# The opening of a fused Fourier-mixing and ELU kernel: x in five pieces, smaller bias parts, a new order of table passes and X units

## The chip, the cores and the metric

The kernel runs on one core of a Trainium2 chip. A core has a matrix engine (TensorE, PE in the profile; its weight loads are listed as PEld), VectorE (DVE), ScalarE (ACT), GpSimd (POOL) and a queue engine (SyncE, SP), which work side by side, each through its own list of instructions in order, and wait for one another through semaphores. Transfers between the chip's main memory (HBM) and the on-chip memory (SBUF) run on 16 DMA engines; here they are asked for by SP and by POOL. Matrix products land in PSUM, a small memory from which ACT and DVE copy them out.

The metric is the device time of one execution in microseconds (us); smaller is better. Beside it there is a profile of one execution with a record of every instruction.

## The reference

```python
def _attn_ref(x, w_r, w_i, b_r, b_i):          # x: (8, 3008, 256)
    X = np.fft.rfft(x, axis=1)
    Xr, Xi = (X.real.astype(np.float32), X.imag.astype(np.float32))
    Yr = Xr @ w_r - Xi @ w_i + b_r
    Yi = Xr @ w_i + Xi @ w_r + b_i
    lam = 0.01
    Yr = np.sign(Yr) * np.maximum(np.abs(Yr) - lam, 0.0)
    Yi = np.sign(Yi) * np.maximum(np.abs(Yi) - lam, 0.0)
    Y = Yr.astype(np.float64) + 1j * Yi.astype(np.float64)
    return np.fft.irfft(Y, n=x.shape[1], axis=1).astype(np.float32)

def _moe_ref(x, w_in, w_out):                  # x: (24064, 256), d_ff = 2048
    h = x @ w_in
    g = np.where(h > 0.0, h, np.exp(np.minimum(h, 0.0)) - 1.0)
    return (g @ w_out).astype(np.float32)
```

The second function is applied to the first one's output, all 8 batches of 3008 tokens in one row.

## The kernel before

**Stages.** The Fourier transform over 3008 = 47 x 64 points is made as two steps of matrix products, and so is its inverse. For each batch the work is cut into units:

- A (6 units): the first transform step. A unit multiplies four of x's 24 row groups by the table M1, copies PSUM to a bf16 tile and writes that to a DRAM buffer (DA). Reading it back in another order gives Z: four loads of 384 KB in the first batch.
- X (8 units): the second step. A unit takes eight of Z's 32 slices times eight slices of the table M2 (`[96, 32, 2, 48]`), and copies the result to XT. Units 2g and 2g+1 need quarter g of Z and of M2.
- M (12): the product with the weights (`wcat_r`, `wcat_s`), bias and soft threshold; an M unit reads all of XT.
- B (6), with the table M3, through another DRAM buffer (DB), and Y (8), with the table M4: the inverse.
- Then the feed-forward part: `front` (w_in and the exponential), `elu`, `back` (w_out and the output).

**Order.** The order of instructions is the order in which the program emits them. For batch 0 all stages stand in line (the opening, up to about 56 us); from then on the feed-forward part of batch b runs with the stages of batch b+1 put between its steps (`plan`). In the opening PE is given filler products on a constant tile (`idle_pe`, L295 to L298).

**The tables.** In the opening the tables are calculated while x arrives. M2 is made in four groups g of eight slices, each by the same steps: `points(g)` (DVE: L433 and L434 make the phase index, L443 the sign `st`), `phases(g)` (the phase, on DVE at L453 or on ACT at L449), `wraps(g)` (DVE, L463 and L464: minus the nearest whole turn), `sizes(g)` (ACT, L474: absolute value), `signs(g)` (DVE, L468), `sines(g, 0)` and `sines(g, 1)` (ACT, L478). `slot0` (DVE, L487, four instructions) corrects slice 0. M3 is made of v3 (DVE, L559), w3 (DVE, L599 and L600: the same wrap), a3 (ACT, L606), two sines (ACT, L613) and two products (DVE, L617 and L621).

**Queues around the change.** x comes in six pieces of 512 KB, asked for by POOL between the iotas that fill index tiles. SP asks for the bias rows, then writes the six A results, then asks for `w_r` and `w_i`, then for the four quarters of Z, then for the bias in 128 rows (`bias_bc`) and for the first part of w_in. POOL turns the weights into bf16 (L520 to L523) and behind that asks for batch 1's x and for half of w_out (L597, L598).

**Bias.** Every second M unit adds its bias by a product with `bias_p`, a `[128, 512]` bf16 tile whose rows 0, 32 and 64 hold three bf16 parts of the fp32 bias and whose other rows are zero (L189). It is made from `brow`, `[128, 512]` in fp32, into which the bias rows are loaded three times (L301 to L307), with L601 on ACT and L602 and L607 to L610 on DVE.

**Copies.** `evac` (L123) copies PSUM to SBUF on ACT or on DVE. In the opening the A units are copied by ACT (L127), X units 1, 4 and 7 by DVE (L125), the others by ACT. A and X units use two PSUM buffers in turn. The last copy of the X stage is followed by the first M units (`first_M`), the two sines of M3 and, after five M units, the first B unit (L630).

Of the kernel before, what the change touches and what calls it, by code (L numbers as in the profile page):

```python
# [29 lines left out]
def kernel(  # L30
# [92 lines left out]
    def evac(dst, src, on_dve):  # L123
        if on_dve:
            nc.vector.tensor_copy(dst, src)  # L125
        else:
            nc.scalar.copy(dst, src)  # L127

    def unit_A(b, u, alone=False, on_dve=False, ahead=False):
        ci, uu = u // 2, u % 2  # L130
        if uu == 0:
            if ahead and ci > 0:
                A_of[b, ci] = wk2.tile([P, 8, D], BF16, name="Bz", tag="Bz")
            elif alone:
                A_of[b, ci] = wk4.tile([P, 8, D], BF16, name="A", tag="Bs")
            else:
                A_of[b, ci] = wk2.tile([P, 8, D], BF16, name="A", tag="A")
            if ci == 0:
                DA_of[b] = dram.tile([NJ, P, D], BF16, name="DA", tag="DA")
        xt, A = xts[ci], A_of[b, ci]  # L140
        dav = DA_of[b].rearrange("j p d -> p j d")
        ps = unit_ps("aps", alone or ahead)
        for j in range(2):
            nc.tensor.matmul(  # L144
                ps[:, j, :], lhsT=M1[:],
                rhs=xt[:, 4 * uu + 2 * j : 4 * uu + 2 * j + 2, :], start=True, stop=True,
            )
        evac(
            A[:, 4 * uu : 4 * uu + 4, :].rearrange("p n d -> p (n d)"),
            ps[:].rearrange("p a b -> p (a b)"), on_dve,  # L150
        )
        j0 = 8 * ci
        if alone:
            j0 += 4 * uu
            nc.sync.dma_start(dav[:, j0 : j0 + 4, :], A[:, 4 * uu : 4 * uu + 4, :])
        elif uu == 1:
            nc.sync.dma_start(dav[:, j0 : j0 + 8, :], A[:])
# [137 lines left out]
    def idle_pe(n):  # L295

        for _ in range(n):
            nc.tensor.matmul(ips[:], lhsT=busy[:, 0:P], rhs=busy[:], start=True, stop=True)  # L298

    brow, rest = (wk3.tile([P, 2 * D], F32, name="yb", tag="yb") for _ in range(2))  # L300
    nc.vector.memset(brow[:], 0.0)  # L301
    for o, bv in ((0, b_r), (D, b_i)):
        for k in range(3):
            nc.sync.dma_start(
                brow[32 * k : 32 * k + 1, o : o + D],
                bass.AP(tensor=bv.tensor, offset=bv.offset, ap=[[0, 1], [1, D]]),
            )  # L307
    idle_pe(9)
    xts = []
    for ci in range(3):  # L310
        xt = constp.tile([P, 8, D], F32R, name=f"xt{ci}")
        xts.append(xt)
    with tc.tile_pool(name="stagep", bufs=1) as stagep:
        def first_x(u):
            load_x(0, u // 2, 4 * (u % 2), 4 * (u % 2) + 4)

        def col(eng, src, s1, op0, s2=None, op1=None, n=1, dt=F32):
            t = stagep.tile([P, n], dt, name=f"c{len(cols)}")
# [49 lines left out]
        for s0, s1 in ((0, 8), (8, NS)):  # L368
            ss = [[15, s1 - s0]]
            iota("", None, ss + [[-15, K1]], base=384 + 15 * s0, out=mi[:, s0:s1, :, 0])  # L370
            if s0:
                first_x(5)
            iota("", None, ss + [[15, K1]], base=15 * s0, out=mi[:, s0:s1, :, 1])
            if s0 == 0:
                iota("", None, [[0, 1], [-15, K1]], base=480, out=mi[:, 0:1, :, 1])
                first_x(3)
                first_x(4)

        m3i = stagep.tile([P, NV], I32, name="m3i")
        k1t = row("k1t", [P, NV])  # L380
# [45 lines left out]
        a2 = row("a2", [P, NS, 2 * K1])  # L426
        r2 = row("r2", [P, 8, 2 * K1])

        def points(g):

            gs, z = slice(8 * g, 8 * g + 8), slice(0, RZ)
            m_, k_ = mi[z, gs], kv[z, gs]
            dve.tensor_scalar(m_, m_, 63, None, ALU.bitwise_and)  # L433
            dve.scalar_tensor_tensor(  # L434
                k_, m_, float(N1), kk1[z].unsqueeze(1).to_broadcast([RZ, 8, K1, 2]),
                ALU.mult, ALU.add,
            )
            if g == 0:
                dve.scalar_tensor_tensor(
                    kv[z, 0, :, 1], mi[z, 0, :, 1], float(N1), kk1[z, :, 0], ALU.mult, ALU.add  # L440
                )
            kf = k_.rearrange("p s k t -> p s (k t)")
            dve.tensor_scalar(st[z, gs], kf, S // 2 + 0.5, -0.5, ALU.is_gt, ALU.add)  # L443

        def phases(g, on_act=False):
            gs, z = slice(8 * g, 8 * g + 8), slice(0, RZ)
# [13 lines left out]
        def wraps(g):  # L460
            gs, z = slice(8 * g, 8 * g + 8), slice(0, RZ)
            v, r = v2[z, gs], r2[z]
            dve.tensor_scalar(r, v, CMAGIC, -CMAGIC, ALU.add, ALU.add)  # L463
            dve.tensor_tensor(v, v, r, ALU.subtract)  # L464
# [33 lines left out]
        pool.tensor_tensor(v4[:], v4[:], r4[:], ALU.subtract)  # L498

        def fA(u):  # L500
            unit_A(0, u, alone=True)
            if u < 5:
                idle_pe(3)

        points(0)
        phases(0)
        wraps(0)
        for u in range(4):
            fA(u)
        points(1)  # L510
        phases(1, True)
        points(2)
        sizes(0)
        fA(4)
        wraps(1)
        signs(0)
        fA(5)
        nc.sync.dma_start(w_r_f[:], w_r.rearrange("(c p) e -> p c e", p=P))
        nc.sync.dma_start(w_i_f[:], w_i.rearrange("(c p) e -> p c e", p=P))
        pool.tensor_copy(wcat_r[:, :, 0:D], w_r_f[:])  # L520
        pool.tensor_copy(wcat_r[:, :, D : 2 * D], w_i_f[:])
        pool.tensor_scalar(wcat_s[:, :, 0:D], w_i_f[:], -1.0, None, ALU.mult)
        pool.tensor_copy(wcat_s[:, :, D : 2 * D], w_r_f[:])  # L523
        for g in range(4):
            load_Z(0, 8 * g, 8 * g + 8)
        for o, bv in ((0, b_r), (D, b_i)):
            nc.sync.dma_start(
                bias_bc[:, o : o + D],
                bass.AP(tensor=bv.tensor, offset=bv.offset, ap=[[0, P], [1, D]]),
            )  # L530
        sines(0, 0)
        sizes(1)
        phases(2, True)
        dve.tensor_scalar(m3i[:], m3i[:], 63, None, ALU.bitwise_and)
        k3 = row("k3", [P, NV])
        dve.scalar_tensor_tensor(k3[:], m3i[:], float(N1), k1t[:], ALU.mult, ALU.add)
        dve.tensor_scalar(sg3[:], k3[:], S // 2 + 0.5, -0.5, ALU.is_gt, ALU.add)
        points(3)
        phases(3)
        wraps(2)  # L540
        signs(1)
        sines(0, 1)
        sines(1, 0)
        sizes(2)
        sines(1, 1)
        wraps(3)
        signs(2)
        slot0()
        sines(2, 0)
        sizes(3)  # L550
        sines(2, 1)
        signs(3)
        sines(3, 0)
        sines(3, 1)


        full = [P, NV, N2]
        k3b = k3[:].unsqueeze(2).to_broadcast(full)
        dve.scalar_tensor_tensor(  # L559
            v3[:], n2row.unsqueeze(1).to_broadcast(full), 1.0 / S, k3b, ALU.mult, ALU.mult  # L560
        )
        idle_pe(40)

    gatep = ctx.enter_context(tc.tile_pool(name="gatep", bufs=2))
    late2 = ctx.enter_context(tc.tile_pool(name="late2", bufs=2))
# [30 lines left out]
    for ci in range(3):  # L596
        load_x(1, ci)  # L597
    load_w_out(0)  # L598
    nc.vector.tensor_scalar(w3[:], v3[:], CMAGIC, -CMAGIC, ALU.add, ALU.add)  # L599
    nc.vector.tensor_tensor(w3[:], v3[:], w3[:], ALU.subtract)  # L600
    nc.scalar.copy(bias_p[:], brow[:])  # L601
    nc.vector.tensor_tensor(rest[:], brow[:], bias_p[:], ALU.subtract)  # L602
    for u in range(8):
        unit_X(0, u, alone=True, on_dve=u in (1, 4, 7))
        if u == 1:
            nc.scalar.activation(a3[:], w3[:], AF.Abs)  # L606
            nc.vector.tensor_copy(bias_p[32:64], rest[32:64])  # L607
            nc.vector.tensor_copy(bias_p[64:P], rest[64:P])
            nc.vector.tensor_tensor(rest[64:P], rest[64:P], bias_p[64:P], ALU.subtract)
            nc.vector.tensor_copy(bias_p[64:P], rest[64:P])  # L610
        idle_pe(1)
    for o, src, sc, bi in ((1, w3, TURN, 0.0), (0, a3, -TURN, hpi[:])):
        nc.scalar.activation(  # L613
# [289 lines left out]
```

## Time and profile before

| | |
|---|---|
| median of 3 runs | 911.97 us (911.74 to 912.75) |
| the profiled execution | 911.1 us |
| its span on the core | 909.3 us |
| TensorE busy | 887.7 us, 98% of the span |
| granted TensorE clock, mean | 0.999 |
| first, last A unit starts on PE | 5.98, 13.22 us |
| first load of Z issued | 18.26 us |
| first, last X unit starts on PE | 22.62, 29.18 us |
| first M, first B unit starts on PE | 30.01, 35.37 us |

A row of the profile's order of time or chain begins with the start and the length in us from the span's start; then come the engine, the line of the kernel and the operation, what is written and read, the tile's shape, and in brackets the idle time of the engine before it and what ended that. A "q" behind an engine's name means its queue, which issues a transfer or waits. In the table by stretches each engine has its busy us and in brackets the number of its instructions; then come the granted clock, the share of the DMA engines' time and GB/s.

### The profile page before, as it was taken

What the parts mean: (1) busy time and instruction counts of PE and PEld (TensorE: products, weight loads), DVE (VectorE), ACT (ScalarE), POOL (GpSimd) and SP (SyncE); (2) the same over time, 40 slices, a digit from 0 to 9 for tenths busy, and PEclk for the clock granted to TensorE, in tenths of its full rate; (3) what the DMA queues carried; (4) which work ended last, traced back from release to release, by engine and by line L of the source; (5) the groups of instructions that cost most, each with busy time, mean ns of one, the idle gap of its engine ahead of it and who ended that gap; (6) DMA issues with size and microseconds to landing.
All of it is one profiled execution on the core that took longest, in us unless ns stands there. A gap on an engine that the chain in (4) does not pass through costs nothing.

```text
span 909.3 us, 17183 instructions
## 1 busy us (share of the span) xinstructions
PE 887.7 (98%) x6622; PEld 652.0 (72%) x6726; DVE 717.0 (79%) x891; ACT 696.6 (77%) x851; POOL 314.7 (35%) x440
## 2 busy tenths in 40 slices
PE   8889999999999999999999999999999999999997
PEld 3457667876688677886678766787667866777775
DVE  8768778877788778797788877888778877778776
ACT  6668788777878778787787788878887877767664
POOL 7600540333321441405404153033332134443664
PEclk9999999999999999999999999999999999999999
DMA  8997116621283215732166032752228111231011
GB/s 270 309 265 232 47 48 186 209 70 47 83 236 123 71 47 142 192 109 82 58 196 199 24 98 60 207 171 70 70 70 232 29 43 47 79 86 48 24 48 47
DMA packets 90670, 106.24 MB, mean 117 GB/s; under 512 B 5270, under 2 KB 81308, under 8 KB 87228
## 3 DMA queue, kind: packets, MB, share of 16 engines
q1 hardware_dynamic: 84332, 77.62, 30.7%
q0 software_dynamic: 5968, 27.26, 9.1%
q8 instruction: 52, 0.85, 0.4%
q14 instruction: 30, 0.25, 0.1%
q10 hardware_dynamic: 288, 0.26, 0.1%
HBM read 55.32 MB, written 49.81 MB: 116 GB/s over the span
## 4 chain that ended last, share of the span: by engine, by line
PE 85%; DVE 5%; ACT 4%; DMA 3%; issue 2%; SPq 1%; POOL 0%; DVEq 0%; ACTq 0%; POOLq 0%
PE ps_o L774 34%; PE hps L716 33%; PE mps L192 9%; PE yps L282 2%; PE bps L244 2%; PE aps L144 2%; PE xps L175 2%; DMA Bs<-DB 2%; DVE gT L743 1%; DVE Et L755 1%; ACT Et L730 1%; ACT Et L727 1%; ACT Bz L257 1%; DVE osb L785 1%; SPq L792 0%
## 5 line engine op out<-in xcount | busy, mean ns | idle before, releaser
L774 PE MATMUL ps_o<-w_out_r,gT 128*128 128x256 f32 x3008 | 477.1, 301 | 0.2 <-DVE gT L741 0.2
L774 PEld LDWEIGHTS ps_o<-w_out_r,gT 128*128 128x128 f32 x3008 | 403.4, 189 | 50.3 <-DVE osb L785 1.3
L716 PE MATMUL hps<-yT,w_in_s 128*128 128x512 bf16 (+7 forms) x1650 | 382.1, 351 | 6.3 <-DVE gT L743 0.9
L741 DVE SCALAR_TENSOR_TENSOR gT<-Et,hps 128x512 fp32r<-128x512 f32 (+1 forms) x274 | 224.0, 847 | 75.8 <-POOL Et L753 38.8
L743 DVE SCALAR_TENSOR_TENSOR gT<-hps,Et 128x1024 fp32r<-128x1024 f32 x197 | 240.9, 1223 | 16.6 <-PE hps L716 1.4
L716 PEld LDWEIGHTS <-w_in_s 128*128 128x128 bf16 x1728 | 141.6, 98 | 129.0 <-issue 22.0
L730 ACT ACTIVATE Et<-hps 128x1024 f32<-128x1024 f32 x197 | 203.0, 1030 | 11.9 <-PE hps L716 5.4
L753 POOL TENSOR_SCALAR Et<-Et 128x512 f32<-128x512 f32 x189 | 112.5, 613 | 221.4 <-ACT Et L725 221.4
L755 DVE TENSOR_SCALAR Et<-Et 128x1024 f32<-128x1024 f32 x197 | 136.2, 691 | 47.4 <-ACT Et L730 40.5
L210 POOL TENSOR_SCALAR clip<-yb 128x512 f32<-128x512 f32 x84 | 51.6, 614 | 315.4 <-DVE yb L202 277.9
L725 ACT ACTIVATE Et<-hps 128x512 f32<-128x512 f32 x190 | 103.2, 595 | 64.7 <-PE hps L716 63.9
L727 ACT ACTIVATE Et<-hps 128x1024 f32<-128x1024 f32 x84 | 86.2, 1026 | 71.7 <-PE hps L716 70.1
L211 POOL TENSOR_TENSOR Y<-yb,clip 128x512 bf16<-128x512 f32 x84 | 107.2, 1276 | 7.0
L728 ACT ACTIVATE Et<-Et 128x1024 f32<-128x1024 f32 x84 | 88.8, 1058 | 2.7
L202 DVE TENSOR_TENSOR yb<-mps,bias_bc 128x512 f32<-128x512 f32 x89 | 61.3, 689 | 35.8 <-PE mps L192 23.9
L127 ACT CAST XT<-xps 128x768 bf16<-128x768 f32 x61 | 48.7, 799 | 16.2 <-PE xps L175 16.2
L127 ACT CAST yT<-yps 128x752 bf16<-128x752 f32 x63 | 49.7, 788 | 13.4 <-PE yps L282 13.3
L192 PE MATMUL mps<-wcat_r,XT 128*128 128x512 bf16 x180 | 55.6, 384 | 0.8 <-ACT Bz L257 0.3
L192 PE MATMUL mps<-wcat_s,XT 128*128 128x512 bf16 x182 | 54.9, 379 | 0.7
L127 ACT CAST A<-aps 128x1024 bf16<-128x1024 f32 x43 | 43.5, 1014 | 13.0 <-PE aps L144 12.3
L192 PEld LDWEIGHTS <-XT 128*128 128x128 bf16 x384 | 30.8, 98 | 29.6 <-DVE XT L125 0.6
L257 ACT CAST Bz<-bps 128x1024 bf16<-128x1024 f32 x46 | 46.0, 999 | 2.1 <-PE bps L244 2.1
(112 smaller groups left out, 413.5 us busy)
## 6 DMA issues: line engine op xcount, KB each, us to landing
xt<-in_x_dram POOLq DMA_DIRECT2D x21, 1024.0 KB, 7.2
out_dram<-osb SPq DMA_DIRECT2D x158, 128.0 KB
Bs<-DB SPq DMA_DIRECT2D x32, 384.0 KB
DB<-Bz SPq DMA_DIRECT2D x21, 512.0 KB
DA<-A SPq DMA_DIRECT2D x19, 512.0 KB
Z<-DA SPq DMA_DIRECT2D x7, 1152.0 KB
Z<-DA SPq DMA_DIRECT2D x11, 384.0 KB
xt<-in_x_dram POOLq DMA_DIRECT2D x6, 512.0 KB, 5.8
```

The costliest lines, as they stand in the source:

```text
L127: nc.scalar.copy(dst, src)
L192: nc.tensor.matmul(ps, lhsT=XT[:, dt, c, o : o + P], rhs=wm[:, dt, :], start=(not biased and m == 0 and dt == 0), stop=(m == 1 and dt == 1),)
L211: nc.gpsimd.tensor_tensor(Y_of[b, q][:, i, :], yb, clip[:], ALU.subtract)
L716: nc.tensor.matmul(hps[:, s, c0:c1], lhsT=w_in_s[:, dt, ft * P : ft * P + P], rhs=yT_of[b][:, dt, t0 : t0 + c1 - c0], start=(dt == 0), sto ...
L725: nc.scalar.activation(E_[:, s], hps[:, s], AF.Exp)
L727: nc.scalar.activation(E_, hps[:], AF.Relu, scale=-1.0)
L730: nc.scalar.activation(E_, hps[:], AF.Exp)
L741: nc.vector.scalar_tensor_tensor(o, e, -1.0, h, ALU.add, ALU.max)
L743: nc.vector.scalar_tensor_tensor(o, h, 0.0, e, ALU.max, ALU.add)
L753: eng.tensor_scalar(E_[:, s], E_[:, s], 1.0, 0.0, ALU.min, ALU.max)
L755: nc.vector.tensor_scalar(E_, E_, 1.0, -1.0, ALU.min, ALU.add)
L774: nc.tensor.matmul(po[q][:, i_ % 2, :], lhsT=gT[:, s, i_ * P : i_ * P + P], rhs=w_out_r[:, ft, :], start=(ft == 0 and i_ % 2 == 0), stop=( ...
```

## The change

All of it is in the opening of batch 0.

- x is asked for in five pieces: two of 1 MB, one of 512 KB, two of 256 KB.
- The last A unit is copied and written in two halves. A unit 3 is copied by DVE.
- The bias is loaded once as 8 rows of 64, split into three bf16 parts of that shape by five small DVE instructions (`split_bias`), written to a DRAM buffer, and read back into rows 0, 32 and 64 of `bias_p` (`place_bias`, three transfers). POOL clears `bias_p` at the very start.
- SP asks for Z's first two quarters, then the weights, then the other two quarters.
- The signs of groups 1 to 3 (`points(g, pool)`) and w3 go to POOL; group 3's `phases` and the negated copy of `w_i` go to ACT.
- The passes over the M2 table are put in another order; `sizes(0)` and what follows now stand behind all A units. X units 0 to 3 are emitted between the passes of groups 2 and 3, and X units 1, 3, 5 and 7 are copied by DVE. a3 stands behind X unit 6. 29 filler products stand ahead of the X units in place of 40.
- The weights' bf16 copies on POOL stand behind all that.

```diff
+        if alone and u == 5:
+            for j in range(2):
+                c = 4 * uu + 2 * j
+                evac(A[:, c : c + 2, :].rearrange("p n d -> p (n d)"), ps[:, j, :], on_dve)
+                nc.sync.dma_start(dav[:, j0 + c : j0 + c + 2, :], A[:, c : c + 2, :])
+            return
...
-    brow, rest = (wk3.tile([P, 2 * D], F32, name="yb", tag="yb") for _ in range(2))
-    nc.vector.memset(brow[:], 0.0)
-    for o, bv in ((0, b_r), (D, b_i)):
-        for k in range(3):
...
+    BR, BC = 8, 2 * D // 8
+    brow, rest = (wk3.tile([BR, BC], F32, name="yb", tag="yb") for _ in range(2))
+    bpart = wk3.tile([BR, 3, BC], BF16, name="yb", tag="yb")
+    bias_d = dram.tile([3, BR, BC], BF16, name="bias_d", tag="bias_d")
+    for o, bv in ((0, b_r), (BR // 2, b_i)):
+        nc.sync.dma_start(
+            brow[o : o + BR // 2, :],
+            bass.AP(tensor=bv.tensor, offset=bv.offset, ap=[[BC, BR // 2], [1, BC]]),
+        )
+    nc.gpsimd.memset(bias_p[:], 0.0)
+    def split_bias():
+        nc.vector.tensor_copy(bpart[:, 0], brow[:])
+        nc.vector.tensor_tensor(rest[:], brow[:], bpart[:, 0], ALU.subtract)
+        nc.vector.tensor_copy(bpart[:, 1], rest[:])
+        nc.vector.tensor_tensor(rest[:], rest[:], bpart[:, 1], ALU.subtract)
+        nc.vector.tensor_copy(bpart[:, 2], rest[:])
+    def place_bias():
+        for k in range(3):
+            nc.sync.dma_start(
+                bias_p[32 * k : 32 * k + 1, :],
+                bias_d[k : k + 1].rearrange("k r c -> k (r c)"),
+            )
...
-            load_x(0, u // 2, 4 * (u % 2), 4 * (u % 2) + 4)
+            load_x(0, *((0, 0, 8), (1, 0, 8), (2, 0, 4), (2, 4, 6), (2, 6, 8))[u])
...
-            unit_A(0, u, alone=True)
+            unit_A(0, u, alone=True, on_dve=u == 3)
...
         points(0)
         phases(0)
+        split_bias()
         wraps(0)
-        for u in range(4):
+        for u in range(5):
             fA(u)
-        points(1)
-        phases(1, True)
-        points(2)
-        sizes(0)
-        fA(4)
-        wraps(1)
-        signs(0)
+            if u == 2:
+                nc.sync.dma_start(bias_d.rearrange("k r c -> r k c"), bpart[:])
+        points(1, pool)
         fA(5)
+        place_bias()
+        for g in range(2):
+            load_Z(0, 8 * g, 8 * g + 8)
         nc.sync.dma_start(w_r_f[:], w_r.rearrange("(c p) e -> p c e", p=P))
         nc.sync.dma_start(w_i_f[:], w_i.rearrange("(c p) e -> p c e", p=P))
-        pool.tensor_copy(wcat_r[:, :, 0:D], w_r_f[:])
-        pool.tensor_copy(wcat_r[:, :, D : 2 * D], w_i_f[:])
-        pool.tensor_scalar(wcat_s[:, :, 0:D], w_i_f[:], -1.0, None, ALU.mult)
-        pool.tensor_copy(wcat_s[:, :, D : 2 * D], w_r_f[:])
-        for g in range(4):
+        for g in range(2, 4):
             load_Z(0, 8 * g, 8 * g + 8)
...
-        sines(0, 0)
-        sizes(1)
-        phases(2, True)
+        sizes(0)
+        phases(1, True)
...
-        points(3)
-        phases(3)
-        wraps(2)
-        signs(1)
+        signs(0)
+        sines(0, 0)
         sines(0, 1)
+        points(2, pool)
+        wraps(1)
+        phases(2, True)
+        sizes(1)
         sines(1, 0)
...
         slot0()
...
+        signs(1)
+        points(3, pool)
+        wraps(2)
+        pool.tensor_scalar(w3[:], v3[:], CMAGIC, -CMAGIC, ALU.add, ALU.add)
+        pool.tensor_tensor(w3[:], v3[:], w3[:], ALU.subtract)
+        sines(1, 1)
+        phases(3, True)
+        sizes(2)
+        sines(2, 0)
+        idle_pe(29)
+        unit_X(0, 0, alone=True)
+        idle_pe(1)
+        signs(2)
+        wraps(3)
+        unit_X(0, 1, alone=True, on_dve=True)
+        idle_pe(1)
+        sines(2, 1)
+        sizes(3)
+        unit_X(0, 2, alone=True)
+        idle_pe(1)
+        signs(3)
+        sines(3, 0)
+        sines(3, 1)
+        unit_X(0, 3, alone=True, on_dve=True)
+        idle_pe(1)
+        pool.tensor_copy(wcat_r[:, :, 0:D], w_r_f[:])
+        pool.tensor_copy(wcat_r[:, :, D : 2 * D], w_i_f[:])
+        nc.scalar.activation(wcat_s[:, :, 0:D], w_i_f[:], AF.Copy, scale=-1.0)
+        pool.tensor_copy(wcat_s[:, :, D : 2 * D], w_r_f[:])
...
-    nc.vector.tensor_scalar(w3[:], v3[:], CMAGIC, -CMAGIC, ALU.add, ALU.add)
-    nc.vector.tensor_tensor(w3[:], v3[:], w3[:], ALU.subtract)
-    nc.scalar.copy(bias_p[:], brow[:])
-    nc.vector.tensor_tensor(rest[:], brow[:], bias_p[:], ALU.subtract)
-    for u in range(8):
-        unit_X(0, u, alone=True, on_dve=u in (1, 4, 7))
-        if u == 1:
+    for u in range(4, 8):
+        unit_X(0, u, alone=True, on_dve=u in (5, 7))
+        if u == 6:
             nc.scalar.activation(a3[:], w3[:], AF.Abs)
...
```

## The prediction

> **What bounds the kernel now.** I read the busy shares first, then the table by stretches of 10 us, then the chain that ended last between 12 and 36 us, then the order of time around the places where that chain lies on VectorE (DVE).
>
> ```profile
> PE 887.7 (98%) x6622; PEld 652.0 (72%) x6726; DVE 717.0 (79%) x891; ACT 696.6 (77%) x851; POOL 314.7 (35%) x440
> ```
>
> TensorE (PE) is busy 98% of the span and the change adds nothing to it, so only the opening can move, and what the opening gains or loses shifts all that follows. By stretches (engine busy us, then clock, DMA share, GB/s):
>
> ```profile
> 10.00:20.00 10.00, 9.70 (x42) 4.18 (x42) 8.83 (x23) 9.42 (x17) 4.57 (x11) 1.00 0.99 295
> 20.00:30.00 10.00, 7.65 (x83) 4.43 (x82) 9.19 (x15) 6.05 (x10) 7.82 (x8) 1.00 1.04 307
> 30.00:40.00 10.00, 9.60 (x53) 4.18 (x55) 6.53 (x10) 6.33 (x10) 7.11 (x8) 1.00 1.27 386
> ```
>
> From 10 to 20 us PE's work is filler (L298). From 20 to 30, where the X units run, DVE is the busy one, 9.19 of 10 us. The chain (start, us, what) says the same:
>
> ```profile
> 18.77 0.53 DVE a L468
> 19.30 1.35 DVE M L487 x4
> 20.65 0.52 DVE a L468
> 21.16 0.88 DVE Bz L559
> 22.07 0.86 DVE A L599
> ...
> 23.83 1.10 DVE yb L602
> 24.93 0.88 DVE XT L125
> ...
> 29.72 0.97 DVE XT L125
> ...
> 30.73 0.82 PE mps L192 x3
> ```
>
> The last X copy ends on DVE at 30.68 and the M units start behind it. Next, two engines side by side:
>
> ```profile
> 5.41 1.15 DVE L433 TENSOR_SCALAR mi<-mi 96x384 int32<-96x384 int32 x1
> ...
> 5.51 0.83 POOL L337 IOTA mi<- 128x576 int32 x1
> ...
> 9.43 0.35 DVE L433 TENSOR_SCALAR mi<-mi 96x384 int32<-96x384 int32 x1
> ...
> 18.82 0.95 POOL L520 CAST wcat_r<-w_r_f 128x512 bf16<-128x512 f32 x1 [4.97 <-DMA w_r_f<-in_w_r_dram]
> 19.22 1.43 DVE L487 TENSOR_SCALAR M<-M,c 96x24 bf16<-96x24 bf16 x4
> ...
> 23.36 1.03 POOL L523 CAST wcat_s<-w_r_f 128x512 bf16<-128x512 f32 x1
> ...
> 23.83 1.10 DVE L602 TENSOR_TENSOR yb<-yb,bias_p 128x512 f32<-128x512 f32 x1
> ```
>
> L433 takes 1.15 us beside a GpSimd (POOL) iota and 0.35 without one. The four equal L487 take 0.59 and 0.65 beside the casts L520 and L521, and 0.23 each after. L602 takes 1.10 beside L523; a like one (L202) takes 0.69. So a POOL instruction of some 0.60 us costs DVE 0.36 to 0.42 when DVE has work. This is the row that decides below.
>
> The Trainium skill ("SBUF — State Buffer", Who interferes with whom) has a rule that speaks against this change: VectorE and GpSimd share a port pair, and the one that comes second is blocked for the whole instruction. By it a POOL instruction would cost DVE all its length, which gives 914.3 below instead of my 914.0; these rows agree in kind, with about 0.6 of the length.
>
> **The change part by part.** Times are of the profiled execution: span 909.3, 911.1 with what lies around it, 0.9 under the median of 911.97. I work out a shift and add it to the median.
>
> *x in five pieces, and the memset.* The A units start as the half-MB pieces land: 5.98, 7.16, 8.97, 10.37, 11.63, 13.22. POOL now first clears `bias_p` (128x512 bf16). No POOL row shows that; below is a 128x1 memset, 0.10, above a 128x512 tensor_scalar, 0.61; I take the same shape on DVE (L292, 0.49). It lies ahead of all x issues and the first iota. DVE's memset at 1.44 is gone, so M1 isn't later. One x issue fewer (0.7) is worth nothing: the data rate ends this wait. The first MB lands where the second half MB did: 7.16+0.49, about 7.5, if larger pieces move a little faster (365 GB/s at 9 to 10 us with 512 KB, 410 at 30 with 1 MB). The later ones come at about 10.3, 11.6, 12.3, 13.2. With PE taking 1.26 a unit (10.37 to 11.63), units start at 7.5, 8.7, 10.4, 11.6, 12.8, 14.0.
>
> *Last A unit in halves.* Two ACT copies of 0.59 (L254) for one of 1.01: the second ends at about 15.55 (before 14.97) and its 128 KB go out then. Before, the six A writes were behind the x data and Z was asked for at 18.26, 3.3 after the last write's issue. A 256 KB write with little beside it (DB<-A in the chain) takes 2.75; half of one about 2.35. So Z is asked for at 15.6+2.35+0.2, about 18.15. The three `place_bias` issues (0.29 each by L304) and the wait for the bounce buffer stand on SP ahead of Z; they end near 17, inside that wait. If the bounce lands later than 17 they are Z's bound; POOL waits for neither.
>
> *Weights behind half of Z.* Two issues (0.54, 0.49) no longer precede Z, but they lay inside the wait for the A writes: nothing. Z's first half landed at 22.6 and I take 22.4. The third and fourth quarters now stand behind 512 KB, 1.5 us at 350 GB/s: the fourth, 26.9 before, lands at about 28.0. The weights themselves come near 25, in time for their casts.
>
> *Bias parts small.* L602 and L607 to L610 (1.10, 0.42, 0.42, 0.69, 0.69) and L601 on ACT (0.60) go; five 8x64 instructions of about 0.2 come (L402, 128x64, took 0.23), before `wraps(0)`, in time in which DVE now idles. Minus 3.3 on DVE.
>
> *Table passes.* DVE loses three L443 (0.35, to POOL), L599 and L600 (0.85, 0.96, to POOL), one L453 (0.47, to ACT); it gains A unit 3 (1.22 by the 128x1024 copy at 49.23) and one X copy (0.95). But `sizes(0)` now stands behind all A copies on ACT: it starts at 15.5, not 12.62. So `signs(0)` starts at 16.0, not 13.62, and DVE idles 1.1 us before it, and from 10.3 to 12.3 for A unit 3. The DVE order from 16.0, laid end to end with the rows above (L468 0.55, L433+L434 0.98, L463+L464 0.87, L487 0.65 for four, L559 0.95): signs 0, points 2, wraps 1, slot0, v3, signs 1, points 3, wraps 2 to about 22.2; 0.6 waiting for `sizes(2)`; signs 2 and wraps 3 to 24.1; X1 to 25.05; signs 3; X3 to 26.6. From there X4, X5, X6, X7 alternate through two PSUM buffers, with two sines and the -w_i copy (0.60) ahead of X4 on ACT: 3.1 more, 29.7. X6 also needs Z's last quarter, which sets X7's end at 30.3. Without any toll from POOL the X stage ends 0.4 earlier than now.
>
> *POOL's toll.* Between 17.5 and 27 POOL now runs st 2 and st 3 (0.46 each, 384/512 of L753's 0.613), w3 as tensor_scalar 128x768 (0.92) and tensor_tensor (1.91, 1.5 times L231's 1.27), and a cast (0.60): 4.35 us. At 0.6 of their length DVE loses 2.6, of which about 0.1 falls in its wait: 2.5. Bounds: 0 (all in gaps) and 2.85 (rows laid with each blocking in full). X3 then ends at 29.1, X7 at 32.2: +1.5.
>
> *The tail.* a3's Abs (0.84) moves from beside X1 to behind X6's copy. X6's copy ends at 31.4; Abs, then the first M3 sine end at 33.0, and L617 starts there, not at 30.73: +2.3. L202 behind it and POOL's clip and Y follow: Y ends at 37.3 (34.98). The first B unit (35.37) had 0.35 to spare: +1.95. Later M units are at PE's pace, and nothing gives it back. POOL's next x and w_out loads start about 4 us later and drain at about 42.5 (before 39): the first B writes wait for them, the last, at 50.4, not; 0, at most 0.8.
>
> Sum: 911.97 + 1.95 = 913.9, say 914.0.
>
> **The rivals.** (1) POOL's work falls into DVE's gaps. For it: DVE waits 0.6 at `sizes(2)`, and L559 and L600 ran at full speed while POOL's L522 took 3.09. Against: L487, L602. X7 ends at 30.3, M3's sine at 31.15, +0.4 at L617, +0.1 at B: 912.1. With half the toll (1.25): X7 31.0, B +0.8, 912.8. Within 0.2%. (2) Faster: no weights share the A writes' last microsecond, so Z comes early. Every step follows Z only if the table is ready, which it is not: at best, Z 0.6 earlier and no toll, X7 at 29.7 and B -0.1 to -0.5: 911.5. For over 0.2% X7 must end by 28.9, Z's last quarter land by 26.6, 1.4 before my estimate. (3) PE slows: filler now ends at about 20.7 (29 of 0.216) and PE idles to 22.4, again around 25.6 to 28 if the toll is full. In this trace PE ran at 0.427 a matmul from 1.45 to about 5.4 and 0.216 after. As long a slow spell in the M units costs 2 us: 916. For it: two gaps; against: 1.24 us at 25 did nothing, the clock stays 1.00. The Trainium skill ("TensorE: Matmul & The Clock Gate", Part 1) puts the idle window at some 3.4 us; neither gap reaches that.
>
> **How the numbers follow.** 0.2%, 1.8 us, is about what a measurement here can tell from no change. Forecast (toll 2.3 or more, 913.8 to 915): 0.43. Rival 1, up to a toll of 2.3: 0.40. Rival 3: 0.09. Rival 2: 0.08. Slower 0.52, same 0.40, faster 0.08. The likeliest's own range is 913.8 to 915. The range reaches down into rival 1 (911.4, toll 0 and the memset at 0.10) and up to rival 3 (916.2).
>
> **What would show it.** `sizes(0)` at 15.5; X7's copy ending at 32.2; the POOL tensor_tensor of w3 near 24 to 27 with a DVE row beside it 1 us or more too long; L617's counterpart at 33.0. Wrong, if w3's pair on POOL runs while DVE waits anyway, if Z lands after 23, or if PE shows 0.427 matmuls past 22 us.

## The result and the profile after

| | before | after |
|---|---|---|
| median of 7 runs each, same chip (us) | 912.75 (911.74 to 913.48) | 915.31 (913.84 to 917.21) |
| ratio, 95% interval | | 1.0034 (1.0024 to 1.0044) |
| profiled execution: time, span (us) | 911.1, 909.3 | 915.31, 913.5 |
| its granted TensorE clock, mean of the span | 0.999 | 0.992 |

The change made the kernel slower: 2.6 us between the medians, 0.34% or 3.1 us by the ratio. The forecast said 2.0, with 914.0 in a range of 911.4 to 916.2; the median of before is 0.8 us higher here than the 911.97 that the forecast was added to. (The profiled execution of after lies 4.2 over that of before, so its profile shows more loss than the medians do.) The time fell where it was said to fall; what follows asks whether for the reasons given.

The busy shares of the page after:

```profile
PE 894.3 (98%) x6715; PEld 653.8 (72%) x6715; DVE 715.7 (78%) x886; ACT 696.0 (76%) x851; POOL 319.7 (35%) x444
```

PE's busy time is 6.6 us longer than before, but that isn't the change: the trace of before lacks some matmul records (it has 1650 of `front`'s 1728), and in the first 40 us PE is busy 2.3 us less after the change (32.30 for 34.58). The stretches of 10 us show where the loss lies, the first 10 us of before on top and the four of after below (busy us and instructions of PE, PEld, DVE, ACT and POOL, then the granted clock, the DMA share and GB/s):

```profile
0.00:10.00 10.00, 7.63 (x24) 2.75 (x24) 8.21 (x32) 4.05 (x6) 8.72 (x33) 1.00 0.76 240
...
0.00:10.00 10.00, 6.48 (x17) 2.48 (x18) 8.14 (x34) 2.92 (x5) 8.76 (x34) 0.92 0.70 254
10.00:20.00 10.00, 9.56 (x39) 4.44 (x38) 5.44 (x12) 6.49 (x10) 4.73 (x10) 0.91 0.71 219
20.00:30.00 10.00, 7.14 (x56) 4.10 (x55) 8.81 (x17) 6.15 (x12) 7.58 (x5) 0.78 0.92 238
30.00:40.00 10.00, 9.13 (x53) 4.59 (x54) 6.43 (x9) 7.48 (x12) 7.36 (x11) 0.71 0.77 266
```

Before, the clock was 1.00 in all four. Now it is halved in four stretches of 3.41 us, one in the A units and three from 25.5 to 35.7. The chain that ended last, after (start, us, what):

```profile
7.38 0.71 PE aps L144 x2
8.09 0.85 PE ips L304 x3
8.95 0.85 PE aps L144 x2
9.80 1.31 PE ips L304 x3
...
16.09 1.07 ACT A L127 x2
17.17 0.42 ACT a L498
17.59 0.02 issue
17.61 0.61 DVE a L492
...
26.75 0.61 DVE XT L125
27.36 0.17 issue
27.54 2.22 DVE a L492
29.76 0.88 DVE XT L125
30.63 0.04 issue
30.68 0.80 PE xps L181 x8
...
33.64 0.97 DVE XT L125
```

`sizes(0)` (L498) begins behind the A copies at 17.05, the table work on DVE follows, and one `signs` (L492) takes 2.22 us. Then PE, which was never the end of the X stage before, stands in the chain with X units of 0.80 us for 0.50. The order of time beside that long instruction:

```profile
24.66 2.80 POOL L574 TENSOR_SCALAR A<-Bz 128x768 f32<-128x768 f32 x1
...
25.08 0.81 DVE L492 SCALAR_TENSOR_TENSOR a<-a,c,st 96x384 f32<-96x384 f32 x1 [1.08 <-ACT M L502]
...
27.54 2.22 DVE L492 SCALAR_TENSOR_TENSOR a<-a,c,st 96x384 f32<-96x384 f32 x1
27.54 1.81 POOL L575 TENSOR_TENSOR A<-Bz,A 128x768 f32<-128x768 f32 x1
```

The same instruction takes 0.61 alone. It starts with w3's tensor_tensor on POOL and lasts 1.61 longer; beside w3's tensor_scalar it lost 0.20.

| us from the start | before | forecast | after |
|---|---|---|---|
| first A unit on PE | 5.98 | 7.5 | 7.38 |
| last A unit on PE | 13.22 | 14.0 | 15.32 |
| `sizes(0)` | 12.62 | 15.5 | 17.05 |
| Z asked for, first and last quarter landed | 18.26, 22.57, 26.90 | 18.15, 22.4, 28.0 | 19.09, 23.39, 29.56 |
| X7's copy ends | 30.68 | 32.2 | 34.60 |
| L617, after L646 | 30.73 | 33.0 | 34.88 |
| first B unit | 35.37 | 37.3 | 39.81 |

### The profile page after: what moved, and what is told of

It reads as the page before. It is cut to its first block, busy times and chain, and to the rows that moved or that the text cites. A ratio compares the mean times of both kernels' runs of the same rounds, so it can differ in the third digit from the quotient of the medians.

```text
span 913.5 us, 17263 instructions
## 1 busy us (share of the span) xinstructions
PE 894.3 (98%) x6715; PEld 653.8 (72%) x6715; DVE 715.7 (78%) x886; ACT 696.0 (76%) x851; POOL 319.7 (35%) x444
## 4 chain that ended last, share of the span: by engine, by line
PE 85%; DVE 5%; DMA 4%; ACT 3%; issue 2%; SPq 0%; POOL 0%; DVEq 0%; ACTq 0%; POOLq 0%
PE ps_o L803 33%; PE hps L745 33%; PE mps L198 9%; PE yps L288 2%; PE bps L250 2%; PE aps L144 2%; PE xps L181 2%; DMA Bs<-DB 2%; DVE gT L772 1%; DVE Et L784 1%; DMA Z<-DA 1%; ACT Et L759 1%; ACT Bz L263 1%; ACT Et L756 1%; DMA xt<-in_x_dram 1%
## 5 line engine op out<-in xcount | busy, mean ns | idle before, releaser
L745 PE MATMUL hps<-yT,w_in_s 128*128 128x512 bf16 (+4 forms) x1728 | 388.8, 352 | 1.7 <-DVE gT L772 0.9
L208 DVE TENSOR_TENSOR yb<-mps,bias_bc 128x512 f32<-128x512 f32 x89 | 61.4, 689 | 35.7 <-PE mps L198 28.9
L198 PE MATMUL mps<-wcat_r,XT 128*128 128x512 bf16 x192 | 58.6, 386 | 0.5 <-ACT Bz L263 0.3
L198 PE MATMUL mps<-wcat_s,XT 128*128 128x512 bf16 x192 | 57.4, 381 | 0.0
L127 ACT CAST A<-aps 128x1024 bf16<-128x1024 f32 (+1 forms) x43 | 42.7, 995 | 17.2 <-PE aps L144 15.8
L198 PEld LDWEIGHTS <-XT 128*128 128x128 bf16 x384 | 30.9, 98 | 29.9 <-DVE XT L125 1.1
```

What stands on the lines that cost most here:

```text
L198: nc.tensor.matmul(ps, lhsT=XT[:, dt, c, o : o + P], rhs=wm[:, dt, :], start=(not biased and m == 0 and dt == 0), stop=(m == 1 and dt == 1),)
L745: nc.tensor.matmul(hps[:, s, c0:c1], lhsT=w_in_s[:, dt, ft * P : ft * P + P], rhs=yT_of[b][:, dt, t0 : t0 + c1 - c0], start=(dt == 0), sto ...
```

## Experiments

Two theories stood at the start. *Toll*: POOL's work lengthens DVE's instructions beside it, and so DVE's path. *Clock*: PE starves, its clock is halved, and slow units hold up the rest. A third, *Z*, came up with the second set. Each run was timed beside the kernel before on the same chip, in 5 to 11 executions. The a runs change the changed kernel (a2 builds on a1, a3 and a4 on a2), the b runs the kernel before, c1 builds on b1. All in one table: the clock is the mean over the executions (a stretch of 3.41 us at half speed takes 0.0019 off it; the last 0.5 to 3.6 us of every profiled execution are at half speed too), the last two columns (us) are of one profiled execution each:

| run | ratio to before (95%) | clock | X7's copy ends | first B |
|---|---|---|---|---|
| before | 1 | 0.9988 | 30.68 | 35.37 |
| after | 1.0034 (1.0024 to 1.0044) | 0.9936 | 34.60 | 39.81 |
| a1_fill_start | 1.0016 (1.0007 to 1.0025) | 0.9945 | 33.13 | 37.83 |
| a2_fill_both | 1.0021 (1.0010 to 1.0031) | 0.9986 | 32.74 | 37.44 |
| a3_no_w3 | 1.0007 (0.9996 to 1.0018) | 0.9987 | 32.03 | 36.72 |
| a4_w3_dve | 1.0014 (1.0004 to 1.0023) | 0.9986 | 32.04 | 36.74 |
| b1_bias | 0.9983 (0.9974 to 0.9992) | 0.9986 | 30.65 | 35.35 |
| b2_zorder | 1.0040 (1.0027 to 1.0052) | 0.9966 | 33.02 | 39.44 |
| b3_both | 1.0015 (1.0006 to 1.0024) | 0.9962 | 32.07 | 38.10 |
| a5_six | 1.0024 (1.0015 to 1.0034) | 0.9948 | 33.46 | 39.14 |
| a6_w_first | 1.0035 (1.0023 to 1.0047) | 0.9957 | 32.32 | 37.18 |
| a7_three_undone | 1.0013 (1.0001 to 1.0025) | 0.9979 | 31.95 | 36.65 |
| c1_bias_x5 | 0.9978 (0.9968 to 0.9987) | 0.9989 | 30.98 | 35.68 |
| a8_early_sizes | 1.0018 (1.0005 to 1.0030) | 0.9979 | 32.21 | 36.90 |

**Filler at the start.**

```diff
-    idle_pe(9)
+    idle_pe(18)
```

> The changed kernel with the filler matmuls ahead of the A units 18 instead of 9, so that PE is at work until about 7.2 us, when the first x piece lands, instead of stopping at 5.3. Clock theory (PE's clock is halved after a stretch of 3.4 us in which PE was too little at work, and the slow A units hold up all that follows): no half clock at 8.4 to 11.8 us, sizes(0) on ACT at 14.3 to 15.2 instead of 17.05, the first Z quarter lands at 21.5 to 22.6 instead of 23.4, X7's copy ends 0.7 to 2 us before 34.6, and the time is 0.7 to 2 us under the changed kernel's (+0.6 to +1.9 against the kernel before). Toll theory (POOL's work on VectorE's port is what costs): sizes(0) may come earlier, the end of X7's copy and the time stay within 0.4 us of the changed kernel's (+2.2 to +3).

Its stretches at the start (columns as above):

```profile
5.13:8.54 3.41, 3.40 (x16) 1.50 (x15) 3.27 (x11) 0.48 (x1) 3.15 (x9) 1.00 1.07 428
8.54:11.95 3.41, 3.41 (x17) 1.52 (x15) 1.98 (x8) 2.55 (x3) 2.83 (x13) 1.00 1.13 386
```

The changed kernel had 1.33 busy of the first stretch and 0.50 of the clock in the second. With PE kept at work the clock stays whole, `sizes(0)` starts at 15.58 (a little later than said) and `signs(0)` at 16.15 instead of 17.61, Z's first quarter lands at 21.30 (a little earlier than said), X7's copy ends 1.5 earlier, and half of the loss is gone (1.0016; the two intervals only just overlap). That is the clock theory's forecast. In the X stage the clock is still halved twice. The mean clock is only 0.0009 above the changed kernel's, half a stretch: so the first stretch can't be halved in every execution of the changed kernel, or the X stage took some of the gain back.

**Filler in the X stage too**, the second pair of lines behind each X unit:

```diff
-        idle_pe(29)
+        idle_pe(38)
...
-        idle_pe(1)
+        idle_pe(3)
```

> The same, and the filler ahead of the X units 38 matmuls instead of 29, and 3 instead of 1 behind each X unit, so that PE isn't idle there either. Clock theory: no half clock before 36 us, X matmul groups at 0.50 and not 0.80, X7's copy ends at 31 to 32.3, L617's counterpart starts at 31.5 to 33, the time is within -0.5 and +0.9 of the kernel before. Toll theory: the X copies are bound by VectorE, X7's copy ends at 32.3 or later with the clock whole, and the time stays 1.5 to 2.5 us over the kernel before.

The clock was whole and X units took 0.50, but X7's copy ended only 0.4 earlier (32.74), and the time did not fall further (1.9 us over the kernel before by the ratio). By its numbers this is the toll theory's forecast. But PE itself was in the way: three filler matmuls make an X unit 0.99 on PE, and the last ones follow each other at that pace (26.25, 27.24, then 29.26, 30.25, 31.24): the cure cost what it saved. So neither the toll nor the clock in the X stage was tested cleanly by this.

**w3 left out, and w3 on DVE.** a3 drops the two POOL instructions (it leaves out the wrap: M3's sines read v3 at a smaller scale, so M3 holds other values); a4 puts them on DVE:

```diff
-        pool.tensor_scalar(w3[:], v3[:], CMAGIC, -CMAGIC, ALU.add, ALU.add)
-        pool.tensor_tensor(w3[:], v3[:], w3[:], ALU.subtract)
...
     load_w_out(0)
+    nc.vector.tensor_scalar(w3[:], v3[:], CMAGIC, -CMAGIC, ALU.add, ALU.add)
+    nc.vector.tensor_tensor(w3[:], v3[:], w3[:], ALU.subtract)
     for u in range(4, 8):
```

> a2_fill_both without the two w3 instructions, which stand on POOL there (the wrap of M3's argument is left out: M3's sines read v3, at a small scale). Toll theory: signs 3 on VectorE takes 0.6 and not 2.2, X7's copy ends 1.6 to 2 us earlier than in a2_fill_both, and the time is 1.3 to 2 us lower. Rival (the X units wait for Z or for ACT, and the toll falls into waiting): X7's copy and the time move by 0.3 us or less.

> a2_fill_both with the two w3 instructions on VectorE again, ahead of X4 (0.85 and 0.96 us there by the trace of before). Toll theory: VectorE is charged about what it was by POOL, so X7's copy ends within 0.4 us of a2_fill_both's and the time is within 0.4. Rival (the toll falls into waiting): X7's copy ends 1 to 1.8 us later than in a2_fill_both.

`signs(3)` in a2_fill_both and in a3_no_w3:

```profile
26.12 2.22 DVE L492 SCALAR_TENSOR_TENSOR a<-a,c,st 96x384 f32<-96x384 f32 x1
```

```profile
26.43 0.60 DVE L492 SCALAR_TENSOR_TENSOR a<-a,c,st 96x384 f32<-96x384 f32 x1
```

The toll is real: 1.62 us on one instruction, gone with w3. But X7's copy comes only 0.71 earlier, not 1.6 to 2, and a4, where DVE itself does the work (0.55 and 0.96 there), ends at the same 32.04. From X3 on (26.56) a3 and a4 were held by the X units' filler, 0.99 apart, so this is the toll's worth beside that cover, not its upper bound; X3's copy, ahead of that cover, ends 1.15 earlier (28.06 for 29.21). The weights' casts also move up into the place of w3 on POOL, and `signs(2)` beside them takes 0.90 in a3 and 1.06 in a4 where it took 0.81: part of the toll came back. In X7's copy neither run met a forecast: a3's 0.71 lies between the toll theory's 1.6 to 2 and the rival's 0.3, and a4's was to stay within 0.4 of a2's or come later. The times agree in sign (1.0021 to 1.0007), with intervals that overlap.

**Two parts alone, and both.** Built on the kernel before. b1 has the small bias parts, with the clearing of `bias_p` behind POOL's iotas and `place_bias` behind Z on the queue:

```diff
+        nc.gpsimd.memset(bias_p[:], 0.0)
...
         points(2)
+        split_bias()
         sizes(0)
...
+        place_bias()
         sines(0, 0)
...
-    nc.scalar.copy(bias_p[:], brow[:])
-    nc.vector.tensor_tensor(rest[:], brow[:], bias_p[:], ALU.subtract)
...
-            nc.vector.tensor_copy(bias_p[32:64], rest[32:64])
-            nc.vector.tensor_copy(bias_p[64:P], rest[64:P])
-            nc.vector.tensor_tensor(rest[64:P], rest[64:P], bias_p[64:P], ALU.subtract)
-            nc.vector.tensor_copy(bias_p[64:P], rest[64:P])
```

b2 has the last A unit in halves and this order:

```diff
-        nc.sync.dma_start(w_r_f[:], w_r.rearrange("(c p) e -> p c e", p=P))
-        nc.sync.dma_start(w_i_f[:], w_i.rearrange("(c p) e -> p c e", p=P))
-        for g in range(4):
+        for g in range(2):
             load_Z(0, 8 * g, 8 * g + 8)
+        nc.sync.dma_start(w_r_f[:], w_r.rearrange("(c p) e -> p c e", p=P))
+        nc.sync.dma_start(w_i_f[:], w_i.rearrange("(c p) e -> p c e", p=P))
+        for g in range(2, 4):
+            load_Z(0, 8 * g, 8 * g + 8)
```

> The kernel before with one part of the change alone: the bias split in 8 rows (split_bias on VectorE ahead of sizes(0), the clearing of bias_p on POOL behind the iotas, place_bias behind Z on the queue). Theory (VectorE sets the end of the X stage, and L602 and L607 to L610, 3.3 us, are on its path): X7's copy ends at 29.0 to 29.9 instead of 30.68, L617's counterpart starts at 30 to 30.6 behind M3's sines, the time is 0.2 to 1.4 us lower. Rival (Z's last quarter or the X buffers set it): X7's copy ends at 30.3 or later and the time is within 0.3 us.

> The kernel before with one other part alone: the last A unit in halves, and the weights asked for behind half of Z (their casts follow the same order on POOL). Theory of the prediction: the first Z quarter lands 0 to 0.6 us earlier than 22.57, the last about 1 us later than 26.9, and VectorE hides both: the time is within 0.4 us of the kernel before. Rival (Z sets the X stage): X7's copy ends 0.5 us or more later and the time is 0.5 to 1.2 us higher.

> b1_bias and b2_zorder together, which leaves out of the change the five x pieces and the new order of the table passes. Theory: Z's last quarter, at about 28, now sets X6 and X7; X7's copy ends at 29.5 to 30.3, the time is 0 to 0.8 us under the kernel before. If it is as low as b1_bias, the weights behind half of Z cost nothing even without VectorE's cover.

b1 is faster by 0.17%. Its profiled execution does not show where: there Z was asked for at 18.92 (0.66 later than before), its last quarter landed at 28.54 (26.90), and the chain ends on it, with DVE idle 1.33 before X7's copy. DVE's part of the theory is seen, the end of X7 at 29.0 to 29.9 is not (30.65, as the rival said); the gain, 1.6 us and a little above what the theory said, stands in the medians alone.

b2 is the surprise: slower by 0.40%, at least as much as the whole change (the intervals overlap, and b2 has five executions). Its chain, and its stretches:

```profile
20.54 0.46 SPq L170
21.00 0.04 issue
21.05 9.05 DMA Z<-DA
30.09 0.05 issue
30.14 0.82 PE xps L181 x8
```

```profile
22.95:26.36 3.41, 2.29 (x34) 1.46 (x31) 3.33 (x6) 3.02 (x4) 0.61 (x1) 1.00 1.07 281
26.36:29.78 3.42, 1.29 (x18) 0.85 (x18) 2.09 (x3) 0.47 (x2) 3.02 (x4) 1.00 0.74 174
29.78:33.19 3.41, 2.85 (x20) 1.68 (x21) 1.10 (x2) 2.54 (x4) 2.81 (x4) 0.50 0.77 211
33.19:36.61 3.42, 3.20 (x8) 1.22 (x9) 2.38 (x3) 0.17 (x1) 1.25 (x1) 0.50 1.02 378
```

Z's third and fourth quarters land at 28.17 and 30.09 (before 25.58 and 26.90): 2.6 and 3.2 us later, 0.46 of it because Z was asked for that much later (18.72) in this execution. PE waits 2.60 at once, is busy 1.29 of 3.42 us, and the clock is halved from 29.78 to 36.61, through half of X and the first M units. X7's copy ends 2.3 later; by the first B unit it is 4.1. Z, not VectorE, set the end there; its price was above the rival's. The weights, which also come later here, did not: their last bf16 copy ends at 29.45, the first M unit starts at 32.24.

b3 stands between, outside its forecast of 0 to 0.8 us under the kernel before: the small bias doesn't hide the order's loss, and 0.50 busy of a stretch (1.70 of 3.41) was again followed by half the clock.

**Six x pieces again.**

```diff
-            load_x(0, *((0, 0, 8), (1, 0, 8), (2, 0, 4), (2, 4, 6), (2, 6, 8))[u])
+            load_x(0, u // 2, 4 * (u % 2), 4 * (u % 2) + 4)
...
```

> The changed kernel with x in six pieces again, and nothing else undone. Clock theory: PE stops at 5.3 and starts again near 6.5, so the clock stays whole from 8.4 to 11.8 us, sizes(0) starts at 15 to 16.2 and not 17.05, the clock is still halved in the X stage, and the time is 0.5 to 2 us under the changed kernel's. Rival (the size of the pieces is of no account, the late A stage comes from the memset and the copies): sizes(0) at 16.7 or later, the time within 0.4 us of the changed kernel's.

PE starts at 6.1, the clock is whole in the A units, `sizes(0)` starts at 15.90, and the time is 0.9 us lower (1.0024 against 1.0034): the clock theory's numbers at their lower end, though the two intervals overlap. With five pieces and filler (a1) it is 1.0016, so the pieces don't look bad as such; PE's wait for the first MB does.

**Weights ahead of Z in the changed kernel; three costs out together.** a6 undoes the order alone. a7 has that, w3 on DVE as in a4, and more filler:

```diff
-        for g in range(2):
-            load_Z(0, 8 * g, 8 * g + 8)
         nc.sync.dma_start(w_r_f[:], w_r.rearrange("(c p) e -> p c e", p=P))
         nc.sync.dma_start(w_i_f[:], w_i.rearrange("(c p) e -> p c e", p=P))
-        for g in range(2, 4):
+        for g in range(4):
             load_Z(0, 8 * g, 8 * g + 8)
```

```diff
-    idle_pe(9)
+    idle_pe(18)
...
-        idle_pe(29)
+        idle_pe(34)
...
-        idle_pe(1)
+        idle_pe(2)
```

> The changed kernel with the weights asked for ahead of all of Z again, and nothing else undone. Theory Z (the 512 KB of weights between the halves of Z make its second half late, PE starves, its clock is halved): the third and fourth Z quarters land 1.5 to 3 us earlier against the first than in the changed kernel (4.7 and 6.2 us behind it there), the clock stays whole or loses one window less behind 22 us, and the time is 1.5 to 3 us under the changed kernel's. Theory VectorE (in the changed kernel VectorE is late by itself, through the late A stage and the stretched signs 3, so Z's second half waits for it): Z lands earlier, X5 still waits for X3's copy, and the time is within 0.6 us of the changed kernel's.

> The changed kernel with the three suspected costs taken out together: 18 filler matmuls at the start and two behind each X unit with 34 ahead of them (clock), the weights ahead of Z, and w3 on VectorE. If these three are the whole of the loss, X7's copy ends at 30 to 31 and the time is 0.3 to 1.5 us under the kernel before, since the small bias stays in. If what is left is the new order of the table passes (sizes(0) behind all A copies), X7's copy ends at 31.3 or later and the time is 0.3 to 1.5 us over it.

a6 is as slow as the change (1.0035). By the medians that is theory VectorE, and X5 still waits for X3's copy (29.10, 29.15). But Z's second half did come closer to the first, as theory Z said, and the mean clock is 0.0021 higher. Its profiled execution, the fastest of nine at 913.0, shows what was traded: the last quarter lands at 28.38 and not 29.56, but the first at 24.26 and not 23.39, since the weights now lie ahead of it, and the first X units are later. (That execution also kept its clock in the A units, with the same instructions there as in the changed kernel: its last A unit starts at 13.79, so its X7 can't be compared with the changed kernel's 34.60.)

a7 keeps 1.0013. Six of its eleven executions had a clock of 0.998 or more and took 911.9 on average, five had 0.996 or 0.997 and took 914.9. So in the same program one or two half-speed stretches more go with 3.0 us; whether they cause all of it isn't shown, since a late Z costs time and can halve the clock too (b2). With a whole clock the loss is gone, though not the bias's gain made. X7's copy at 31.95 pointed to the tables' order as the rest; that was the last experiment:

```diff
         for u in range(5):
+            if u == 4:
+                sizes(0)
             fA(u)
...
         points(1, pool)
+        phases(1, True)
         fA(5)
...
-        sizes(0)
-        phases(1, True)
```

> a7_three_undone with sizes(0) on ACT ahead of the fifth A copy and phases(1) ahead of the last, as in the kernel before (a7_three_undone has both behind all A copies, at 15.45). Theory tables (what is left of the loss is that order): sizes(0) starts at 11.4 to 12.6, signs(0) on VectorE at 14 to 15 and not 16.02, X1's copy starts at 24 to 25 and not 25.58, X7's copy ends at 30 to 31.2 instead of 31.95, and the time is 0.5 to 1.6 us under a7_three_undone's. Rival (the X stage of that kernel waits for Z, or for ACT and VectorE in the X units themselves): signs(0) comes earlier, X7's copy ends within 0.4 us of 31.95 and the time is within 0.4.

`sizes(0)` starts at 11.37 and `signs(0)` at 14.40, as said, and nothing is won: X7's copy ends at 32.21. The chain of this run:

```profile
17.82 6.62 DMA Z<-DA
24.45 0.05 issue
24.49 0.52 PE xps L181 x8
```

Now Z's first quarter takes 6.62 us to land, and the earlier table waits for it. The rival holds, and the tables' order is not what was left. In the three runs that ask for the weights 1.0 us ahead of Z, behind `place_bias` (a6, a7, a8), the first quarter takes 5.7 to 6.6 us from asking to landing; in the kernel before, where they are asked for 2.9 us ahead, 4.3, and in the changed kernel, where they follow, 4.3. Most of the 1.4 to 2.3 us more is the weights' own transfer: `w_i` lands 2.4 to 2.6 us behind the request for Z in these three and 1.2 behind it in the kernel before, and Z's first quarter 3.3 to 4.1 after `w_i`, where it was 3.1. The rest is open.

**What beats both.** b1 with the five pieces of x, and the filler moved:

```diff
-            load_x(0, u // 2, 4 * (u % 2), 4 * (u % 2) + 4)
+            load_x(0, *((0, 0, 8), (1, 0, 8), (2, 0, 4), (2, 4, 6), (2, 6, 8))[u])
...
-    idle_pe(9)
+    idle_pe(18)
...
-        idle_pe(40)
+        idle_pe(34)
...
```

> b1_bias with x in five pieces and 18 filler matmuls at the start (34 instead of 40 behind the A units). In b1_bias X7 waited for Z's last quarter (28.54). Theory: with the pieces x has landed at 12.3 and not 13.7, Z is asked for 0.6 to 1.2 us earlier, its last quarter lands at 26 to 27.5, X7's copy ends at 28.7 to 30, and the time is 0.4 to 1.5 us under b1_bias, 2 to 3.3 us under the kernel before. Rival (the five pieces bring nothing that Z's waiting does not take back): within 0.4 us of b1_bias.

0.9978: 2.0 us faster than before, the fastest here. Against b1 (0.9983, same build but the pieces and filler) the difference is within the intervals, so what the pieces add isn't shown. Its profiled execution missed the steps that were said (last quarter at 27.72, X7's copy at 30.98, later than before) and had the clock halved once, from 24.86 to 28.28; as in b1, the gain stands in the medians alone.

## Why the prediction was right, point by point

The number held: 2.6 to 3.1 us for a forecast of 2.0. In the sum behind it VectorE's path came out nearly as said, and a term for the clock was missing. Two of the three signs that the prediction named for being wrong were there: Z landed after 23 (23.39), and PE showed half-speed matmuls past 22 us (0.43 a filler). `sizes(0)`, X7's copy and L617 came 1.6, 2.4 and 1.9 later than said.

- *Memset and pieces.* 0.52 measured for 0.49, first unit at 7.38 for 7.5: right. The last A unit was wrong, 15.32 for 14.0, and with it `sizes(0)`, 17.05 for 15.5. The step that failed is the dismissal of rival 3: PE's gap from 5.3 to 7.38 halves the clock in the A units. The sum's own 7.5 for the first unit implied this gap, but rival 3 looked only at gaps behind 20 us. With the gap filled (a1) the last A unit came at 13.9 and `sizes(0)` at 15.6, the forecast's own times.
- *Rival 3, at 0.09.* It happened, and is the largest single effect that the runs show: half of the loss at the start alone (1.0034 to 1.0016, by intervals that just overlap). The argument against it was a gap shorter than an idle window. The Trainium skill ("TensorE: Matmul & The Clock Gate", Part 1) names at least one idle window of some 3.4 us; the length of the steps agrees (3.41 in the trace), but no whole idle one was needed: single gaps of 2.08 at the start, of 1.11 and 0.97 in the X stage, and of 2.60 in b2 were enough.
- *Weights behind half of Z*, costed at +1.1 on the last quarter and 0 on the time: the most mis-sized term. Alone it (with the last A unit in halves) gave 2.6 to 3.2 on the quarters, 2.1 to 2.7 counted from the request for Z, and 0.40% on the time. The 350 GB/s taken for it weren't there: b2 moved 281 and then 174 in those stretches. In the changed kernel undoing it gave nothing; its profile suggests why, since the other order makes Z's first half late.
- *Small bias*, 3.3 us off DVE: right in sign; alone worth 0.17%, 1.6 us.
- *POOL's toll*, 2.5: about 2.2 in the trace (1.61 and 0.20 on `signs`, 0.19 on each of two L488, 0.74 for 0.56). That the size fits is luck: POOL's five instructions took 8.7 us and not 4.35, and cost DVE a quarter of their length and not 0.6. Its effect on DVE's path, which ends with X3's copy, is borne out: said for 29.1, it ended at 29.16 in a1, whose A units had the whole clock. The Trainium skill ("SBUF — State Buffer", Who interferes with whom) has the second instruction blocked for the whole first one: L575 agrees (1.61 of 1.81), L574 does not (0.20 of 2.80), so the measurement decides.
- *Tail*, 0.8 beyond X7: 0.28 (34.60 to 34.88). X7's copy itself was so late that the Abs and the first sine were nearly done.
- *Rival 1*, up to a toll of 2.3: by its size the toll lies at this border, but it fell on DVE's path and not into gaps.
- *Rival 2*, faster: not this change, but b1 and c1 show that its bias part, without the new order of Z, is.

So X7's copy was late by 3.9 in the profiled execution, not 1.5, and the 2.4 between them can be placed. X3's copy ended at 30.62, in a1 at 29.16: 1.5 through the slow A stage. From there to the end of X7's copy the forecast took 3.1; it was 3.98 in the changed kernel, a1 and a5, whose clock was halved there, and 3.22 in a6, where it was whole from 29.45 on: 0.8 to 0.9 through the slow X units. By these comparisons both are the clock, which the forecast put at nothing. That the time still came out near is in part luck: the two profiled executions differ by 4.2 us, the medians by 2.6, because the profiled one of before was a fast one. What stays open is what a7 and a8 keep, 0.1 to 0.2%; in a7 it goes with the executions whose clock was halved.

## What to carry to other kernels

When a change lets PE wait, look at how much PE is busy in each 3.4 us around the wait, not at whether one gap is long: a half-speed stretch can cost nearly as much again as the wait (1.5 us of X7's copy behind the gap of 2.08 at the start), and a few filler matmuls are cheap, as long as they don't pace the units themselves. Before a load is moved ahead of another, ask which engine will starve if the second comes 2 to 3 us late, and whether what hides it today is something that the same change removes. A forecast that meets the time is not yet a right one: undo its parts one by one.

## What the hardware showed that was not expected

Cut into the trace's own steps, the PE busy time before each change of the clock is telling. The changed kernel:

```profile
5.02:8.43 3.41, 1.33 (x8) 0.56 (x6) 3.27 (x11) 0.30 (x1) 3.20 (x8) 1.00 1.07 428
8.43:11.85 3.42, 3.42 (x10) 1.66 (x9) 1.80 (x8) 1.72 (x2) 2.83 (x14) 0.50 1.14 394
22.09:25.50 3.41, 1.53 (x20) 0.94 (x19) 2.26 (x6) 2.70 (x5) 2.38 (x2) 1.00 1.07 287
25.50:28.91 3.41, 2.47 (x21) 1.70 (x21) 3.38 (x5) 2.30 (x5) 3.33 (x2) 0.50 0.99 238
28.91:32.33 3.42, 2.70 (x26) 1.94 (x25) 2.53 (x3) 1.72 (x3) 3.04 (x6) 0.50 0.08 21
32.33:35.74 3.41, 3.21 (x17) 1.37 (x15) 1.95 (x3) 3.10 (x4) 2.40 (x4) 0.50 0.93 259
```

And the kernel before, which kept its clock:

```profile
23.07:26.49 3.42, 1.99 (x31) 1.37 (x29) 3.38 (x5) 2.42 (x4) 3.36 (x6) 1.00 1.05 249
```

A stretch that was busy 1.33 or 1.53 of 3.41 (39 and 45%) is followed by one at half speed; 1.99 (58%) is not. Over the first 40 us of all fourteen profiled executions every stretch at 45% or less led to half speed, all at 51% or more kept it, and between them both occur. Once halved there, the clock came back only behind a stretch at 88% or more: 72, 79 and 84% were not enough (2.47, 2.70 above, 2.85 in b2). The share isn't all of it, though: at the very start matmuls also come 0.43 apart, and in b3 a first stretch busy 79% was enough to end that. The grid of stretches lies differently in each execution (its first edge between 4.1 and 6.2 us), so the same program is halved in one and not in the next: a6, with the changed kernel's opening, had 1.74 busy (51%) in its stretch from 5.56 and kept its clock. This is probably the wider spread of the changed kernel (913.84 to 917.21).

POOL's time hangs on the operation: tensor_scalar with a comparison took 1.5 to 1.6 for 96x384, whether DVE was idle for more than half of it (15.30 to 16.81) or busy nearly throughout (19.17 to 20.78), and with two additions 2.80 for 128x768, where 0.61 for 128x512 with a minimum and maximum had led the forecast to 0.46 and 0.92. Of the 2.80 DVE was busy 2.3, so that one need not be POOL's own pace. For POOL can be the one that pays: the copy of `w_i` times -1 (128x512) took 3.09 in the kernel before, beside a DVE that was busy for 3.02 of it, and 1.52 in b3, where DVE was idle. The prediction read that row only for DVE, which ran at full speed beside it.
